# Gated attention and token-MLP mix: shared PSUM banks, a choice of evacuation engine and new planned costs, three weight slots, and MLP1 ahead of the late projections

## The chip, the cores and the metric

The kernel runs on one core of one Trainium2 chip. The metric is the device time of one execution in microseconds, as the median of several executions. The span in a profile (first to last instruction) is about 2 us shorter than that time.

A single core has no die to compare with, so runs are compared by their granted TensorE clock. Runs over 1.5% above the fastest were marked slow and are left out of the ratios. A ratio below is the mean time of one kernel's fast runs over that of the other's fast runs of the same rounds on the same chip, so it is not quite the ratio of the medians quoted beside it, and neither is corrected for the clock. Where a difference is small, runs at like clock are compared as well.

Names: PE is TensorE, PEld its weight loads, DVE is VectorE, ACT is ScalarE, POOL is GpSimd.

## The reference

Sequence S = 2048, width D = 448, 16 heads of 28, 4 segments of 512 rows, MLP width F = 1792. All tensors are bf16.

```python
x = A_x
g = sigmoid((x * gate_w).sum(-1, keepdims=True))
a = attention_with_memory(x, wq, wk, wv, wo, beta)     # below
b = token_mlp(x, w1, b1, w2, b2)                       # below
return g * a + (1 - g) * b

# attention_with_memory, for each segment s (q, k, v are projections of x, per head):
logits = qs @ ks.T * Dh**-0.5 + causal_mask
a_dot  = softmax(logits) @ vs
a_mem  = phi(qs) @ M / (phi(qs) @ z + 1e-6)            # phi(t) = t + 1 if t > 0 else exp(t)
o      = sigmoid(beta) * a_mem + (1 - sigmoid(beta)) * a_dot
M, z   = M + phi(ks).T @ vs, z + phi(ks).sum(0)        # segment s + 1 needs segment s
# ... output projection with wo

# token_mlp mixes along the sequence, so it needs only the normalised x:
h = layernorm(x)
u = gelu(h.T @ w1 + b1)      # MLP1: 14 tiles of 16 matmuls, 128x448 each
y = (u @ w2 + b2).T          # MLP2: 16 tiles of 14 matmuls, 128x448 each
```

What matters here is that the two branches meet only at the end. The MLP is pure TensorE work with light post-processing. Attention is done in 16 units (4 segments by 4 groups of 4 heads) and keeps DVE, ACT and GpSimd busy.

## The kernel before

The kernel records its operations with their reads, writes, cost estimate and priority. A list scheduler then simulates five in-order engines and fixes the order of each engine's instructions at build time. On the chip each engine runs its list in that order and waits on semaphores. So a wrong cost estimate does not break anything: it only puts an instruction at a place in its list where it will wait, and everything behind it on that engine waits too.

The planner, cut:

```python
HOP = 80.0                                   # one figure for every engine-to-engine signal
SWITCH = 110.0

class Sched:
    def op(self, eng, fn, reads=(), writes=(), ..., cost=100.0, lat=None, prio=None, mode=None, nbytes=0):
        ...
        o.cost = cost
        o.lat = {"PE": 180.0, "ACT": 95.0}.get(eng, 0.0) if lat is None else lat
        o.prio = (self.now if prio is None else prio, o.idx)
    def plan(self):
        # ... cut: take the engine that can start first; on it, the ready operation of lowest prio
            o.start = t
            free[e] = t + c
            ...
                o.end = t + c + o.lat
            # ... cut
                r = (o.end + HOP) if (isdep and x.eng != o.eng) else (o.end if isdep else free[e])

def pe_cost(*cols):                 return sum(max(c, 64) / 2.4 + 3.0 for c in cols)
def act_cost(n, sbuf=False, ptr=0): return n / 1.2 + (100.0 if sbuf else 80.0) + 90.0 * ptr
def dve_cost(n, rate=1.0):          return n / rate / 0.96 + 150.0
def pool_cost(n):                   return n / 1.2 + 320.0
```

PSUM banks and engines are fixed when the operation is recorded. Scores own banks 0 to 3, the probability-times-V product (P·V) bank 4, memory term and output projection bank 5, projections alternate between 5 and 6 after the start, the MLP uses 7 (later 6 and 7):

```python
    P_BASE, P_ATT, P_PROJ, P_WO, P_M1, P_M2 = 0.0, 100.0, 200.0, 300.0, 400.0, 500.0   # lower goes first
    CTX, MISC = 4, 5

    def do_k(tc, hg):                      # tc: segment, hg: group of heads
        b = next_bank()
        proj_d(wk_pad, R_wkp, hg, tc, b)   # 4 matmuls, prio=P_PROJ + tc
        op("ACT", lambda e: e.activation(ks, bank(b)[:, 0:512], ACT.Copy), ..., cost=act_cost(512), prio=P_BASE)

    def do_q(tc, hg):
        b = next_bank()
        proj_d(wq_pad, R_wqp, hg, tc, b)
        op("DVE", lambda e: e.tensor_copy(qs, bank(b)[:, 0:512]), ..., cost=dve_cost(512), prio=P_BASE)
```

The clamp of phi, on DVE, and the causal mask, on GpSimd:

```python
        op("DVE", lambda e: e.tensor_scalar_min(kphi[:, p, :], kphi[:, p, :], 1.0), ..., cost=dve_cost(512, 4), ...)
        ...
            op("POOL", lambda e, d=d: e.affine_select(d, d, pattern=[[0, 4], [1, 128]], ...), ..., cost=750, prio=pr)
```

The MLP weights stream through seven slots, four of which reuse memory that the projections own until they are finished, so all projections must come before MLP1 can go far:

```python
    slots = [wown[:, 0, :], wown[:, 1, :], wown[:, 2, :], xTf[:, 0:RING], xTf[:, RING : 2 * RING],
             wqk.rearrange("p a c d -> p (a c d)"), phk.rearrange("p t k -> p (t k)")[:, 0:RING]]
    ...
    def mlp_next():
        i = NFT + NT - len(mlp)
        f_, a = mlp.pop(0)
        f_(a, 7 if i < NB7 else 6 + i % 2)             # bank
        if (i < NFT and i % 2 == 1) or (i >= NFT and (i - NFT) % 2 == 1):
            ring_load()
```

By priority, attention units come first, then projections in segment order, then output projection, MLP1, MLP2. TensorE takes an MLP matmul only when nothing of the rest is ready in the plan.

The softmax here doesn't subtract the row's maximum and nothing guards it: scores larger than these inputs give would overflow.

Of the kernel before, what the change touches and what calls it, by code (L numbers as in the profile page):

```python
# [38 lines left out]
class Op:  # L39
    __slots__ = ("eng", "evspace", "fn", "deps", "order", "is_event", "ev_val", "knowledge", "waits", "name", "idx",  # L40
                 "cost", "lat", "prio", "mode", "start", "end", "pos", "nbytes")
# [3 lines left out]
HOP = 80.0  # L45
SWITCH = 110.0


class Sched:
# [3 lines left out]
    def __init__(self, nc):  # L53
        self.nc = nc
        self.ops = []
        self.per_eng = {e: [] for e in ENGINES}
        self._dma_uid = 0
        self.out_spaces = set()
        self.now = 0.0

    def op(self, eng, fn, reads=(), writes=(), name=None, dma=False, out=False, cost=100.0, lat=None, prio=None,
           mode=None, nbytes=0):
# [4 lines left out]
        o.lat = {"PE": 180.0, "ACT": 95.0}.get(eng, 0.0) if lat is None else lat  # L67
        o.prio = (self.now if prio is None else prio, o.idx)
        o.mode = mode
        o.nbytes = nbytes  # L70
        o.start = o.end = o.pos = None
        if dma:
            self._dma_uid += 1
            o.evspace = "dma_u%d" % self._dma_uid
            o.is_event = True
        else:
            o.evspace = eng
# [12 lines left out]
        for r in reads:  # L90
            if r.last_write is not None:
                need(r.last_write)
            if r.psum and eng != "PE":
                for rd in r.reads:
                    if rd.eng != eng and rd.eng != "PE":
                        need(rd)
# [16 lines left out]
    def plan(self):  # L113
        import heapq
# [3 lines left out]
        ready = [0.0] * len(self.ops)  # L118
# [6 lines left out]
        chan = 0.0  # L125
        waiting = {e: [] for e in ENGINES}
        avail = {e: [] for e in ENGINES}
        for o in self.ops:
            if left[o.idx] == 0:
                heapq.heappush(waiting[o.eng], (0.0, o.prio, o))  # L130
        done = 0
        line = []
        while done < len(self.ops):
            best = None
            for e in ENGINES:
                w, a = waiting[e], avail[e]
                while w and w[0][0] <= free[e]:
                    t, p, o = heapq.heappop(w)
                    heapq.heappush(a, (p, o))
                if a:  # L140
                    t = free[e]
                elif w:
                    t = w[0][0]
                else:
                    continue
                if best is None or t < best[0]:
                    best = (t, e)
            t, e = best
            if not avail[e]:
                while waiting[e] and waiting[e][0][0] <= t:  # L150
                    _, p, o = heapq.heappop(waiting[e])
                    heapq.heappush(avail[e], (p, o))
            _, o = heapq.heappop(avail[e])
            c = o.cost
            if e == "PE" and o.mode != mode:
                c += SWITCH
                mode = o.mode
            o.start = t
            free[e] = t + c
# [3 lines left out]
            else:  # L163
                o.end = t + c + o.lat
            o.pos = done
            line.append(o)
            self.per_eng[e].append(o)
            done += 1
            for x in succ[o.idx]:
                isdep = any(d is o for d in x.deps)  # L170
                r = (o.end + HOP) if (isdep and x.eng != o.eng) else (o.end if isdep else free[e])
# [3 lines left out]
                if left[x.idx] == 0:  # L175
                    heapq.heappush(waiting[x.eng], (ready[x.idx], x.prio, x))
# [52 lines left out]
def pe_cost(*cols):  # L229
    return sum(max(c, 64) / 2.4 + 3.0 for c in cols)  # L230


def act_cost(n, sbuf=False, ptr=0):
    return n / 1.2 + (100.0 if sbuf else 80.0) + 90.0 * ptr


def dve_cost(n, rate=1.0):
    return n / rate / 0.96 + 150.0


def pool_cost(n):
    return n / 1.2 + 320.0


def build_kernel(nc, X, WQ, WK, WV, WO, BETA, W1, B1, W2, B2, GW, OUT):
    sch = Sched(nc)
# [22 lines left out]
    def bank(b):  # L269
        return ps[:, b, :]  # L270


    wown = sb([128, 3, RING])
# [48 lines left out]
    xTf = xT.rearrange("p c t -> p (c t)")  # L322
    slots = [wown[:, 0, :], wown[:, 1, :], wown[:, 2, :], xTf[:, 0:RING], xTf[:, RING : 2 * RING],
             wqk.rearrange("p a c d -> p (a c d)"), phk.rearrange("p t k -> p (t k)")[:, 0:RING]]
# [13 lines left out]
    R_own = R("own", 3)  # L338
# [11 lines left out]
    slot_res = [[R_own[0]], [R_own[1]], [R_own[2]], [r for t in R_xT for r in t], [r for t in R_xT for r in t],  # L350
                [R_wkp, R_wqp], [r for t in R_phk for r in t]]
    R_slot = R("slot", 7)
# [32 lines left out]
    def ring_load():  # L385
# [4 lines left out]
        r = k % 7  # L390
        first = slot_res[r] if k < 7 else []
        if k < 7:
            op("SP", lambda e: e.dma_start(slots[r].rearrange("p (t f) -> p t f", t=NT),
                                           w1v[:, :, k * 256 : k * 256 + 256]),
               reads=[R_wv, R_gw], writes=[R_slot[r]] + first, name=f"ldw1_{k}", dma=True, cost=500,
               nbytes=1048576)
        else:
# [3 lines left out]
               writes=[R_slot[r]] + first, name=f"ldw2_{j}", dma=True, cost=500, nbytes=917504)  # L401
# [31 lines left out]
    P_BASE, P_ATT, P_PROJ, P_WO, P_M1, P_M2 = 0.0, 100.0, 200.0, 300.0, 400.0, 500.0  # L433


    rr = [0]
    banks_now = [[0, 1, 2, 3, 4, 5, 6, 7]]

    def next_bank():
        rr[0] += 1  # L440
        return banks_now[0][(rr[0] - 1) % len(banks_now[0])]

    def fn_warm(e):
        last = None
        for _ in range(18):
            last = e.matmul(bank(7)[:, 0:512], warm[:, 0:128], warm[:, 0:512], start=True, stop=True,  # L446
# [3 lines left out]
    op("PE", fn_warm, reads=[R_ob[0]], writes=[R_bank[7]], name="warm", mode="f", cost=3600, prio=-1)  # L450
# [3 lines left out]
       reads=R_P[0], writes=[R_wkp], name="padk", cost=dve_cost(1792, 2), prio=P_BASE)  # L454

    def pad_q():
        op("DVE", lambda e: e.tensor_copy(wq_pad.rearrange("p c (h j) -> p (c h) j", j=32)[0:CK, :, 0:DH],
                                          wq_nat.rearrange("p c (h j) -> p (c h) j", j=DH)[0:CK]),
           reads=R_P[1], writes=[R_wqp], name="padq", cost=dve_cost(1792, 2), prio=P_BASE)

    def transposes(tc):
        for half in range(2):
            b = next_bank()
            tb = bank(b).bitcast(BF16)

            def fn(e, half=half, tb=tb):
# [9 lines left out]
            op("PE", fn, reads=R_x[4 * tc : 4 * tc + 4] + [R_ident], writes=[R_bank[b]], name=f"trx{tc}_{half}",  # L476
               mode="f", cost=8 * 66, prio=P_PROJ)
            dst = xT[0:CK, 2 * half : 2 * half + 2, tc * 512 : tc * 512 + 512]
            src = tb[0:CK, :].rearrange("p (c t) -> p c t", c=2)
            if tc == 0 and half == 0:  # L480
                op("ACT", lambda e, dst=dst, src=src: e.activation(dst, src, ACT.Copy), reads=[R_bank[b]],
                   writes=[R_xT[tc][half]], name=f"xTcp{tc}_{half}", cost=act_cost(1024), prio=P_BASE)
            else:
                op("DVE", lambda e, dst=dst, src=src: e.tensor_copy(dst, src), reads=[R_bank[b]],
                   writes=[R_xT[tc][half]], name=f"xTcp{tc}_{half}", cost=dve_cost(1024, 2), prio=P_PROJ + tc - 150)

    def proj_d(w_pad, R_w, hg, tc, b):
        def fn(e):
# [7 lines left out]
        op("PE", fn, reads=R_xT[tc] + [R_w], writes=[R_bank[b]], name=f"prd{tc}_{hg}", mode="f",  # L496
           cost=pe_cost(512, 512, 512, 512), prio=P_PROJ + tc)

    def do_k(tc, hg):
# [4 lines left out]
           reads=[R_bank[b]], writes=[R_kT[hg][tc]], name=f"cpk{tc}_{hg}", cost=act_cost(512), prio=P_BASE)  # L504

    def do_kphi(tc, hg):
# [5 lines left out]
           reads=[R_kphi[p]], writes=[R_kphi[p]], name=f"mk{tc}_{hg}", cost=dve_cost(512, 4), prio=P_PROJ + tc)  # L512
        op("DVE", lambda e: e.scalar_tensor_tensor(kphi[:, p, :], ks, 0.0, kphi[:, p, :], op0=ALU.max, op1=ALU.add),  # L513
           reads=[R_kT[hg][tc], R_kphi[p]], writes=[R_kphi[p]], name=f"phk{tc}_{hg}", cost=dve_cost(512),
# [5 lines left out]
    def do_q(tc, hg):  # L520
# [3 lines left out]
        op("DVE", lambda e: e.tensor_copy(qs, bank(b)[:, 0:512]), reads=[R_bank[b]], writes=[R_qT[hg][tc]],  # L524
           name=f"cpq{tc}_{hg}", cost=dve_cost(512), prio=P_BASE)

    def do_qphi(tc, hg):
# [5 lines left out]
           reads=[R_phq[hg][tc]], writes=[R_phq[hg][tc]], name=f"mq{tc}_{hg}", cost=dve_cost(512, 4),  # L533
           prio=P_PROJ + tc)
        op("DVE", lambda e: e.scalar_tensor_tensor(ph, qs, 0.0, ph, op0=ALU.max, op1=ALU.add),  # L535
           reads=[R_qT[hg][tc], R_phq[hg][tc]], writes=[R_phq[hg][tc]], name=f"phq{tc}_{hg}", cost=dve_cost(512),
           prio=P_PROJ + tc)

    def do_v(t):
        b = next_bank()  # L540

        def fn(e):
            last = None
            for c in range(NCT):
# [4 lines left out]
        op("PE", fn, reads=R_xT[t // 4] + [R_wv, R_gw], writes=[R_bank[b]], name=f"prt{t}", mode="f",  # L549
           cost=pe_cost(449, 449, 449, 449), prio=P_PROJ + t // 4)  # L550
        op("ACT", lambda e: e.activation(vaug[:, t, :].rearrange("p (h c) -> p h c", h=H)[:, :, 0:DH],  # L551
                                         bank(b)[:, 0:D].rearrange("p (h c) -> p h c", h=H), ACT.Copy),
           reads=[R_bank[b]], writes=[R_v[t]], name=f"cpv{t}", cost=act_cost(448), prio=P_BASE)
        op("ACT", lambda e: e.activation(gth[:, t : t + 1], bank(b)[:, D : D + 1], ACT.Tanh, scale=0.5),
           reads=[R_bank[b]], writes=[R_gth[t]], name=f"gt{t}", cost=act_cost(1), prio=P_BASE)

    def do_mst(s):
        b = next_bank()

        def fn(e):  # L560
# [9 lines left out]
        op("PE", fn, reads=R_phk[s] + R_v[4 * s : 4 * s + 4], writes=[R_bank[b]], name=f"mst{s}", mode="f",  # L570
           cost=16 * 64, prio=P_PROJ + s)
        mps = bank(b)[:, 0:512].rearrange("p (g c) -> p g c", g=NHG)
        if s == 0:
            op("DVE", lambda e: e.tensor_copy(mst_f32[:], mps), reads=[R_bank[b]], writes=[R_mstf], name="msta0",
               cost=dve_cost(512), prio=P_BASE)
        else:
            op("DVE", lambda e: e.tensor_tensor(mst_f32[:], mps, mst_f32[:], op=ALU.add), reads=[R_bank[b], R_mstf],
# [350 lines left out]
```

## Time and profile before

| | kernel before |
|---|---|
| time, median (lowest to highest) | 210.63 us (209.08 to 210.69), 3 runs |
| profiled span, mean granted clock | 208.8 us, 0.984 |
| busy: PE, DVE, ACT, POOL | 91%, 73%, 65%, 35% |
| matmuls after the last P·V group | 202, in 38.4 us |

Lines of the kernel before that the profile names: L491 is the q and k projection, L711 is P·V, L757 the output projection, L774 MLP1, L799 MLP2, L804 the final combination, L524 the q copy, L511 and L513 phi on DVE, L688 the mask on GpSimd.

From the page of the kernel before: the first lines are the busy times and the busy share in tenths in 40 slices of 5.2 us each, then the chain of work that ended last by engine, then three groups (busy us, mean ns of one | idle before, and its main releaser).

```profile
span 208.8 us, 3428 instructions
...
PE 189.4 (91%) x1359; PEld 84.8 (41%) x1359; DVE 153.4 (73%) x301; ACT 136.7 (65%) x181; POOL 73.7 (35%) x93
...
PE   7799989967996799789778899999999999999994
...
DVE  2779999999999899999999577777657571222222
...
PEclk9999999999999799969999999999999999999999
...
PE 46%; DVE 40%; ACT 7%; POOL 3%; issue 2%
...
L774 PE MATMUL t<-t 128*128 128x448 bf16 x224 | 52.6, 360 | 1.7 <-ACT t L781 1.7
L799 PE MATMUL t<-t 128*128 128x448 bf16 x224 | 43.4, 353 | 0.0
L491 PE MATMUL t<-t 112*128 112x512 bf16 x128 | 31.8, 389 | 6.9 <-DVE t L524 5.0
```

PE seems full at 91%, yet that row stretches matmuls: the groups show 360 and 353 ns for one of 448 columns. The Trainium skill, "Perfetto Trace Analysis", section "Identifying the Most-Contended Engine", comes to the same conclusion: matmul busy time is a bad measure of how close one is to the limit. Its reason, that pipelined matmuls look smaller in a trace, isn't what these groups show; here they look longer than the 189 ns found next. The last lines of the chain of waits of the kernel before show what a matmul really takes (start, us, what, number of instructions):

```profile
166.93 0.66 PE t L711 x16
167.58 5.59 PE t L799 x29
173.18 3.03 PE t L757 x16
176.20 29.71 PE t L799 x157
...
205.94 0.68 DVE t L804
```

157 matmuls in 29.71 us are 189 ns each, half of the 353. From such back-to-back rates the prediction below works out some 178 us of true TensorE work, so about 27 us of the span are gaps. The chain also shows the tail: after the last P·V group (it ends at 167.6 us) there are 29 + 16 + 157 = 202 matmuls and nothing else.

The busy time of each engine in stretches of the kernel before (us of the stretch; then busy us of PE, PEld, DVE, ACT, POOL with counts; granted clock; DMA share; GB/s):

```profile
core 0: us, PE busy (x) PEld busy (x) DVE busy (x) ACT busy (x) POOL busy (x), PEclk, DMA share, GB/s
40.00:50.00 10.00, 7.13 (x58) 2.72 (x57) 9.69 (x25) 7.81 (x10) 3.43 (x4) 1.00 0.13 26
60.00:70.00 10.00, 7.34 (x45) 2.72 (x45) 9.72 (x20) 8.29 (x13) 2.74 (x4) 1.00 0.13 26
88.00:90.00 2.00, 0.43 (x3) 0.25 (x4) 1.93 (x6) 2.00 (x3) 0.13 (x1) 1.00 0.41 78
92.00:94.00 2.00, 2.00 (x13) 0.59 (x11) 2.00 (x4) 1.05 (x2) 1.60 (x2) 0.50 0.92 242
130.00:140.00 10.00, 9.76 (x77) 4.17 (x75) 7.44 (x13) 9.75 (x12) 6.21 (x7) 1.00 0.47 135
180.00:190.00 10.00, 10.00 (x54) 5.19 (x53) 2.19 (x4) 0.00 (x0) 0.00 (x0) 1.00 0.14 46
```

At 40 to 50 and at 60 to 70 us DVE is 97% busy and PE 71 to 73%: TensorE waits for DVE. At 130 to 140 PE and ACT are both nearly full. At 180 to 190 there is only PE, and DVE and ACT have no work. The limit moves from DVE to ACT and PE to PE alone.

One more thing in the timeline of the kernel before (start, duration, engine, line, operation): the same clamp of 128x512 elements takes two different times.

```profile
41.24 0.29 DVE L511 TENSOR_SCALAR t<-t 128x512 bf16<-128x512 bf16 x1
...
41.57 1.18 POOL L688 TENSOR_SCALAR_AFFINE_SELECT t<-t 128x512 bf16<-128x512 bf16 x1 [2.52 <-ACT t L684]
...
42.17 0.72 DVE L511 TENSOR_SCALAR t<-t 128x512 bf16<-128x512 bf16 x1
```

The first clamp runs without a GpSimd instruction beside it and takes 0.29 us. The second starts while the mask L688 runs and takes 0.72. Over the 12 clamps of that line the least is 0.25 and the most 1.37 us. The Trainium skill, "SBUF — State Buffer", section "Who interferes with whom", describes an exclusive lock on a port pair that DVE and GpSimd share; this trace agrees in effect.

### The profile page before, as it was taken

Reading aid. Unit: us, or ns where it says so; the run is one execution under the profiler, and the core shown is the slowest. Engines: PE = TensorE matmul, PEld = TensorE weight load, DVE = VectorE, ACT = ScalarE, POOL = GpSimd, SP = SyncE. Lnnn points to the kernel's source line nnn. Section 1 sums busy time; section 2 is a strip of 40 time slices with the busy share of each in tenths; the row PEclk is TensorE's granted clock in tenths of the full one; section 3 lists DMA queues with packets and bytes.
Section 4 is the critical chain, followed back from the end, with each engine's and each line's share of the span. In section 5 each row is a group of like instructions: output and inputs, shape, how many; then the busy total and the mean of one; then the engine's idle time right before and its main releaser. Section 6 shows DMA issues by size and latency. Waiting matters only on the chain.

```text
span 208.8 us, 3428 instructions
## 1 busy us (share of the span) xinstructions
PE 189.4 (91%) x1359; PEld 84.8 (41%) x1359; DVE 153.4 (73%) x301; ACT 136.7 (65%) x181; POOL 73.7 (35%) x93
## 2 busy tenths in 40 slices
PE   7799989967996799789778899999999999999994
PEld 2446434323532244333333344334343455555551
DVE  2779999999999899999999577777657571222222
ACT  2262799995998779959859799998899405000000
POOL 8100058450424123744473652763745520000000
PEclk9999999999999799969999999999999999999999
DMA  5999901020202079774407153260606160111111
GB/s 157 255 286 287 276 8 25 5 50 12 41 0 50 19 209 223 202 206 110 121 0 202 36 141 99 80 176 3 176 0 179 51 191 22 49 44 44 44 44 44
DMA packets 42451, 21.75 MB, mean 104 GB/s; under 512 B 7876, under 2 KB 42436, under 8 KB 42436
## 3 DMA queue, kind: packets, MB, share of 16 engines
q1 hardware_dynamic: 41496, 21.30, 38.5%
q10 hardware_dynamic: 940, 0.24, 0.5%
q8 instruction: 10, 0.16, 0.3%
q14 instruction: 5, 0.04, 0.1%
HBM read 18.13 MB, written 1.84 MB: 96 GB/s over the span
## 4 chain that ended last, share of the span: by engine, by line
PE 46%; DVE 40%; ACT 7%; POOL 3%; issue 2%
PE t L799 20%; PE t L491 6%; PE t L757 5%; PE t L774 4%; ACT t L684 4%; DVE t L513 3%; DVE t L734 3%; DVE t L725 3%; DVE t L535 3%; PE t L711 3%; DVE t L744 3%; PE t L446 3%; DVE t L639 3%; DVE t L736 3%; DVE t L724 2%; DVE t L511 2%
## 5 line engine op out<-in xcount | busy, mean ns | idle before, releaser
L684 ACT ACTIVATE t<-t 128x2048 bf16<-128x2048 f32 (+1 forms) x48 | 77.6, 1616 | 5.3 <-PE t L675 5.0
L688 POOL TENSOR_SCALAR_AFFINE_SELECT t<-t 128x512 bf16<-128x512 bf16 x64 | 47.6, 750 | 70.6 <-ACT t L684 69.3
L774 PE MATMUL t<-t 128*128 128x448 bf16 x224 | 52.6, 360 | 1.7 <-ACT t L781 1.7
L799 PE MATMUL t<-t 128*128 128x448 bf16 x224 | 43.4, 353 | 0.0
L491 PE MATMUL t<-t 112*128 112x512 bf16 x128 | 31.8, 389 | 6.9 <-DVE t L524 5.0
L774 PEld LDWEIGHTS t<-t 128*128 128x128 bf16 x224 | 20.4, 99 | 24.7 <-issue 8.1
L804 DVE SCALAR_TENSOR_TENSOR t<-t 128x448 bf16<-128x448 f32 x16 | 10.8, 677 | 26.5 <-PE t L799 26.4
L799 PEld LDWEIGHTS t<-t 128*128 128x128 bf16 x224 | 21.6, 98 | 20.3 <-issue 0.5
L738 POOL TENSOR_TENSOR t<-t 128x512 bf16<-128x512 f32 x12 | 17.5, 1456 | 26.5 <-DVE t L736 26.5
L491 PEld LDWEIGHTS t<-t 112*128 112x128 bf16 x128 | 11.1, 99 | 22.0 <-DVE t L524 5.8
L675 PE MATMUL t<-t 28*128 28x512 bf16 (+3 forms) x256 | 17.5, 306 | 1.2 <-ACT t L684 1.2
L763 ACT ACTIVATE t<-t 128x448 bf16<-128x448 f32 x16 | 11.7, 731 | 9.7 <-PE t L757 9.6
L757 PE MATMUL t<-t 128*128 128x448 bf16 x64 | 14.3, 355 | 4.0 <-DVE t L724 3.8
L725 DVE STREAM_TRANSPOSE t<-t 128x512 f32<-128x512 f32 x16 | 11.4, 710 | 5.9 <-PE t L711 5.9
L744 DVE STREAM_TRANSPOSE t<-t 128x512 bf16<-128x512 bf16 x16 | 11.3, 706 | 4.6 <-POOL t L738 4.4
L545 PE MATMUL t<-t 112*128 112x449 bf16 x64 | 14.5, 361 | 0.0
L711 PE MATMUL t<-t 128*32 128x512 bf16 (+3 forms) x256 | 12.3, 316 | 1.4 <-POOL t L688 1.3
L551 ACT ACTIVATE t<-t 128x448 bf16<-128x448 f32 x16 | 8.7, 562 | 7.4 <-PE t L545 7.4
L675 PEld LDWEIGHTS t<-t 28*128 28x128 bf16 x256 | 5.2, 92 | 19.3 <-ACT t L684 12.4
L524 DVE CAST t<-t 128x512 bf16<-128x512 f32 x16 | 10.8, 678 | 1.5 <-PE t L491 1.4
L503 ACT ACTIVATE t<-t 128x512 bf16<-128x512 f32 x16 | 10.0, 651 | 2.9 <-PE t L491 2.9
L623 DVE BATCH_NORM_STATS2 t<-t 128x6 f32<-128x448 bf16 x16 | 9.5, 597 | 2.6 <-DMA t<-in_A_x_dram 2.6
(75 smaller groups left out, 214.9 us busy)
## 6 DMA issues: line engine op xcount, KB each, us to landing
t<-in_B_w_dram SPq DMA_DIRECT2D x7, 1024.0 KB, 7.2
t<-in_B_w_dram SPq DMA_DIRECT2D x8, 896.0 KB, 5.2
out_dram<-t SPq DMA_DIRECT2D x16, 112.0 KB, 1.7
t<-in_A_x_dram SPq DMA_DIRECT2D x3, 448.0 KB, 9.3
t<-in_A_wk_dram SPq DMA_DIRECT2D x1, 392.0 KB, 5.0
t<-in_A_wq_dram SPq DMA_DIRECT2D x1, 392.0 KB, 6.9
t<-in_A_wv_dram SPq DMA_DIRECT2D x1, 392.0 KB, 8.2
t<-in_A_wo_dram SPq DMA_DIRECT2D x4, 98.0 KB
```

Of the source, the lines that this page charges most:

```text
L491: last = e.matmul(bank(b)[:, 0:512], w_pad[0:CK, c, hg * 128 : hg * 128 + 128], xT[0:CK, c, tc * 512 : tc * 512 + 512], start=(c == 0), st ...
L545: last = e.matmul(bank(b)[:, 0 : D + 1], xT[0:CK, c, t * 128 : t * 128 + 128], wvx[0:CK, c, :], start=(c == 0), stop=(c == NCT - 1), skip_ ...
L675: last = e.matmul(bank(hl)[:, c0 : c0 + w_], kT[r, hg, s * 512 + j * 128 : s * 512 + j * 128 + 128], qT[r, hg, s * 512 + 128 * j : s * 512 ...
L684: op("ACT", lambda e: e.activation(pv, ps[:, 0:4, 0:w], ACT.Exp, scale=SCALE), reads=R_bank[0:4], writes=[R_P[u % 2][f]], name=f"exp{n}", ...
L688: op("POOL", lambda e, d=d: e.affine_select(d, d, pattern=[[0, 4], [1, 128]], compare_op=ALU.is_ge, fill=0.0, base=0, channel_multiplier=- ...
L711: last = e.matmul(bank(CTX)[32 * hl : 32 * hl + 32, 128 * j : 512], vaug[:, 4 * s + j, 32 * h : 32 * h + 32], pv[:, hl, c0 : c0 + w_], sta ...
L725: dv(lambda e: e.transpose(t2[:, 0, :], bank(CTX)[:, 0:512]), [R_bank[CTX]], [R_tt[tb][0]], "ta", 720)
L738: op("POOL", lambda e: e.tensor_tensor(o, t2[:, 0, :], t2[:, 1, :], op=ALU.add), reads=R_tt[tb], writes=[R_ob[tb]], name=f"o{u}", cost=140 ...
L744: dv(lambda e: e.transpose(oT[:, hg, s * 512 : s * 512 + 512], o), [R_ob[tb]], [R_qT[hg][s]], "ot", 700)
L757: last = e.matmul(bank(b)[:, 0:D], oT[:, hg, T * 128 : T * 128 + 128], wo_sb[:, hg, :], start=(hg == 0), stop=(hg == NHG - 1), skip_group_ ...
L774: op("PE", lambda e, st=st: e.matmul(bank(b)[:, 0:D], w1c[:, st, f2 * 128 : f2 * 128 + 128], xh[:, st, :], start=(st == 0), stop=(st == NT ...
L799: op("PE", lambda e, ft=ft: e.matmul(bank(b)[:, 0:D], w2c[:, ft, t2_ * 128 : t2_ * 128 + 128], uT[:, ft, :], start=(ft == 0), stop=(ft == ...
```

## The change

The intent is to fill TensorE's gaps in the first 110 us with MLP work and so shorten the tail. Three things are done for it.

1. **Order.** The projections of segments 2 and 3 get priorities inside the MLP instead of before it, so MLP1 starts earlier. Because the memory of those projections is then not free, the weight slots shrink from seven to three of their own.
2. **Planner resources.** Projections, P·V, memory term, output projection and MLP take a bank from a pool of four (4 to 7) when the plan reaches them, and most PSUM evacuations may go to ACT or DVE, whichever is free first in the plan.
3. **Planner costs.** The cost figures are set nearer to measured ones, engine-to-engine hops get a table, and a new rule lets operations flagged `port` on DVE and GpSimd exclude each other in the plan.

No arithmetic changes. The diff, cut to its core:

```diff
-HOP = 80.0
-SWITCH = 110.0
+HOP = {("PE", "ACT"): 40.0, ("PE", "DVE"): 40.0, ("ACT", "PE"): 58.0, ("DVE", "PE"): 60.0, ... }
+SWITCH = 97.0
+LAT = {"PE": 163.0, "ACT": 120.0, "DVE": 83.0, "POOL": 50.0, "SP": 0.0}
 ...  plan():
+            if o.take is not None:                       # bank given out when the plan reaches the operation
+                b = min((v[0], b) for b, v in banks.items())[1]
+                o.take.bank = b
+                o.deps = o.deps + banks[b][1]
+                banks[b] = (1e18, [])
+            o.eng = e                                     # engine chosen by the plan among o.alts
+            o.fn, c, pt = o.alts[e]
+            if pt:                                        # DVE and GpSimd exclude each other
+                t = max(t, port)
+                port = t + c
 ...
 def act_cost(n, sbuf=False, ptr=0):
-    return n / 1.2 + (100.0 if sbuf else 80.0) + 90.0 * ptr
+    return n / 1.2 + (95.0 if sbuf else 50.0) + 92.0 * ptr
 def dve_cost(n, rate=1.0):
-    return n / rate / 0.96 + 150.0
+    return n / rate / 0.96 + 70.0
 ...
-    slots = [wown[:, 0, :], ..., xTf[:, 0:RING], xTf[:, RING : 2 * RING], wqk..., phk...]
+    slots = [wown[:, i, :] for i in range(NSL)]          # NSL = 3
 ...
+    PRJ = (P_PROJ, P_PROJ + 1, P_M1 + 8.5, P_M2 + 4.5)
 ...
-           cost=pe_cost(512, 512, 512, 512), prio=P_PROJ + tc)
+           cost=pe_cost(512, 512, 512, 512), prio=PRJ[tc])
 ...  do_q():
-        op("DVE", lambda e: e.tensor_copy(qs, bank(b)[:, 0:512]), ...)
+        op("DVE", lambda e: e.tensor_copy(qs, bank(b)[:, 0:512]), **buse(b), ...,
+           alt=("ACT", lambda e: e.activation(qs, bank(b)[:, 0:512], ACT.Copy), act_cost(512)))
 ...  masks:
-               ..., name=f"mask{n}_{c0}", cost=750, prio=pr)
+               ..., name=f"mask{n}_{c0}", cost=590, port=True, prio=pr)
 ...  ln_coef(): the power (rstd) on GpSimd
-            op("POOL", fn, ..., cost=250, prio=P_BASE)
+            op("POOL", fn, ..., cost=2900 if name == "rstd" else 200, prio=P_BASE)
 ...  pv_unit(), wo_tile(), mm1(), mm2():
-    CTX, MISC = 4, 5
+        mb, cb = Bank("pool"), Bank("pool")
```

## The prediction

> **What bounds the kernel now.** The span is 208.8 us, matmul busy 91%, but that row stretches matmuls: the groups show 353 to 360 ns for 448 columns, while in the unbroken run ending the chain of waits 157 take 29.71 us, 189 ns each. The chain's back-to-back rates (189 ns MLP and output projection, 221 for 512-column projections, 193 for V, 0.7 us per probability-times-V group, 0.9 us per unit's scores) over all counts give about 178 us of true TensorE work; with 4 us of start and end the floor is near 182: 27 us are gaps.
>
> In the 10 us windows DVE is 90 to 99% busy from 20 to 110 us while four PE windows are only 71 to 78%; there the chain is nearly all DVE. From 110 to 160 us PE and ACT share the limit (both about 95%), DVE about 74%. From 167.6 us there is PE only: 202 matmuls, 38 us.
>
> **What the change does.** Same arithmetic.
> - Projections of segments 2 and 3 go behind MLP1 and into MLP2. After the last attention unit 118 matmuls remain, 22.3 us instead of 38.2.
> - Evacuations: ACT takes 3 more x-transpose copies and 11 q copies; DVE takes 8 k copies, 7 v copies, 5 GELU halves, 6 gate evacuations. With the group means DVE gains about 7 us (153 to 161), ACT loses about 7 (137 to 130). It helps by timing only.
> - Four shared banks instead of fixed ones remove waits such as TensorE on q copies (5.0 us, weight loads 5.8, in the waits).
> - Three weight slots instead of seven: a 1 MB load lands in 7.2 us, a 0.9 MB one in 5.2; two tiles use a slot for at least 5.3 us, with two slots ahead: nearly no wait.
>
> **Sum along the path.** I cut both orders at each unit's output transpose and add durations (scaled to the busy union, 0.93 on DVE). Before: DVE to unit 8 105 us plus 7 of idle start, then PE 89.5, plus 3: 205, against 208.8 measured, so stalls cost 4. After: DVE to unit 11 119 plus 7, then PE 64.4, plus 3, plus 4 of stalls: 197.5. Planned costs nearer to measured ones should trim stalls. They include DVE-GpSimd exclusion, which the Trainium skill, "SBUF — State Buffer", describes as an exclusive lock on a shared port pair; the trace agrees: the same 512-element clamp takes 0.25 us at best and 0.72 us beside a GpSimd mask.
>
> **Prediction: 196 us, 189 to 205 in 8 of 10.** Faster by over 2%: 0.89; within 2%: 0.09; slower: 0.02.
>
> **What would show it.** A PE-only tail of 22 to 25 us (38 before). DVE over 90% from 20 to about 125 us, then near 65%; DVE total about 161 us, ACT 130. PE busy 94 to 97%. TensorE's waits on q copies under 3 us. No wait over 2 us on a weight load.
>
> **What would make it wrong.** (a) DVE growing more than 7 us through lock conflicts: 200 or over. (b) In-order engines stalling where durations differ from the plan, or units 12 to 15 held by ACT's exponentials with no MLP2 tile to fill: plus 5. (c) The load queue blocked behind a slot, delaying phi transposes or weights: plus 3 to 6. (d) The granted clock, 0.83 in two windows now, dropping in a denser run: plus 2 to 4. (e) DVE keeping pace better than its means: 189.

## More of the kernel before

The mean clock of an execution of this kernel is between 0.975 and 1.0, and the time follows it: over all executions the kernel before took about 209.0 us at clock 1.0, 209.4 at 0.991, 210.6 at 0.984 and 213.5 at 0.976.

The two short stretches at 88 and 92 us show another loss: PE is busy for only 0.43 us of 2, and shortly after the granted clock is 0.50.

## The result, and the profile after

| | before | after |
|---|---|---|
| time, median (lowest to highest) | 209.86 us (208.93 to 210.69), 4 runs | 193.66 us (191.93 to 194.31), 4 runs |
| ratio of fast runs, 95% interval | | 0.9216 (0.9138 to 0.9295) |
| profiled span, clock | 208.8 us, 0.984 | 191.8 us, 0.991 |
| at clock 1.0 | about 209.0 us | 191.93 us (one run) |
| matmuls after the last P·V group | 202, in 38.4 us | 118, in 22.5 us |

The result is correct; the kernel before has one run more here than above, made beside it. The kernel takes 7.8% less time. At clock 1.0 the difference is 17 us (one run of the kernel after); at 0.991 it is about 15.5 (193.9, the mean of three runs, against 209.4).

In the kernel after, L558 is the q and k projection, L788 P·V, L836 the output projection, L856 MLP1, L884 MLP2, L890 the final combination, L550 the copy of transposed x, L675 the tanh of beta. The page of the kernel after, the same parts as before:

```profile
span 191.8 us, 3430 instructions
...
PE 184.2 (96%) x1350; PEld 85.1 (44%) x1359; DVE 157.0 (82%) x313; ACT 134.0 (70%) x169; POOL 74.3 (39%) x93
...
PE   7769999999999999999999999999999999999993
...
DVE  2678987989999998989888997898899998971221
...
PEclk9988999999999999999999999999999999999999
...
PE 87%; DVE 4%; DMA 3%; ACT 3%; issue 1%; ACTq 1%
...
L856 PE MATMUL t<-t 128*128 128x448 bf16 x224 | 48.4, 354 | 0.5 <-DVE t L579 0.2
L884 PE MATMUL t<-t 128*128 128x448 bf16 x224 | 45.1, 353 | 0.1
L558 PE MATMUL t<-t 112*128 112x512 bf16 x128 | 31.6, 396 | 2.7 <-DVE t L550 2.7
```

PE's row is at 9 from the fourth slice to the last but one, and the chain, formerly 46% PE and 40% DVE, is now 87% PE. The projection's idle time on q copies (5.0 us before) is gone; what remains of it is one wait of 2.7 us at the start. DVE's row stays at 7 to 9 from 10 to about 170 us.

The chain of waits of the kernel after, its start and its end:

```profile
1.85 6.63 DMA t<-in_A_beta_dram
8.51 0.22 ACT t L675
...
10.21 0.70 DVE t L550
...
11.05 7.03 PE t L558 x24
...
165.80 0.66 PE t L788 x16
166.45 6.54 PE t L884 x34
172.99 3.03 PE t L836 x16
176.02 12.88 PE t L884 x68
188.92 0.68 DVE t L890
```

The tail after the last P·V group is 34 + 16 + 68 = 118 matmuls in 22.5 us, at the same 189 ns each.

The same windows of the kernel after, with two short ones from its start (columns as before):

```profile
10.00:12.00 2.00, 0.95 (x5) 0.51 (x6) 1.77 (x6) 0.00 (x0) 0.00 (x0) 1.00 1.09 373
12.00:14.00 2.00, 2.00 (x8) 0.79 (x7) 1.28 (x6) 1.24 (x3) 0.00 (x0) 0.63 1.12 301
40.00:50.00 10.00, 10.00 (x90) 4.11 (x89) 9.10 (x19) 9.19 (x11) 4.69 (x6) 1.00 0.16 44
60.00:70.00 10.00, 9.79 (x74) 4.43 (x74) 9.82 (x19) 9.64 (x11) 4.00 (x5) 1.00 0.09 19
130.00:140.00 10.00, 9.95 (x56) 5.01 (x55) 8.63 (x16) 1.75 (x2) 3.67 (x4) 1.00 0.73 172
```

PE is full or nearly so (98 to 100%) where it was 71 to 73%, at about the same DVE load (91 to 98%, against 97). From 130 to 140 us ACT has little to do and DVE is at 86%.

**Where the 17 us came from.** The path can be cut at two places that both chains show. From the first projection to the last matmul the kernel before needs 9.67 to 205.9 us, 196.2 in all, and the kernel after 11.05 to 188.9, 177.9 in all: 18.4 us less. The first projection starts 1.4 us later. The end after the last matmul is 2.9 us in both. The sum is −17.0 us, the difference of the spans. Of the prediction's estimate of 178 us of true TensorE work about 171 lie in that stretch (without the 6.1 us of warm-up and 0.9 of first transposes), so the gaps in it fell from about 25 us to about 7. These gaps include what the half-clock stretches cost: the profiled execution before had two of them (clock 0.984), the one after had one (0.991), so by estimate some 1.7 of the 17 us are the clock.

Attention itself hardly moved: the last P·V group ends at 167.6 us before and at 166.5 after. The gain is the 84 matmuls (202 less 118) that now lie in the gaps before it; at 189 ns they are 15.9 us.

**The one thing that grew.** The start of the chain after shows it. The tanh of beta stands in ACT's list ahead of the first copy of x, and it waits until 8.51 us for the load of beta. DVE's small operations that depend on it are ahead of the other copy (L550). So the projections begin at 11.05 instead of 9.67. In the windows PE is busy for 0.95 us of the 2 from 10 to 12, and the granted clock is 0.63 in the next 2.

### The profile page after: what moved, and what is told of

It reads as the page before. It is cut to its first block, busy times and chain, and to the rows that moved or that the text cites. A ratio compares the mean times of both kernels' runs of the same rounds, so it can differ in the third digit from the quotient of the medians.

```text
span 191.8 us, 3430 instructions
## 1 busy us (share of the span) xinstructions
PE 184.2 (96%) x1350; PEld 85.1 (44%) x1359; DVE 157.0 (82%) x313; ACT 134.0 (70%) x169; POOL 74.3 (39%) x93
## 4 chain that ended last, share of the span: by engine, by line
PE 87%; DVE 4%; DMA 3%; ACT 3%; issue 1%; ACTq 1%
PE t L884 23%; PE t L856 21%; PE t L558 16%; PE t L751 7%; PE t L614 7%; PE t L836 6%; PE t L788 5%; DMA t<-in_A_beta_dram 3%; PE t L638 2%; ACT t L760 2%; PE t L539 1%; DVE t L803 1%; DVE t L604 1%; ACT t L860 1%; PE t L774 0%
## 5 line engine op out<-in xcount | busy, mean ns | idle before, releaser
L764 POOL TENSOR_SCALAR_AFFINE_SELECT t<-t 128x512 bf16<-128x512 bf16 x64 | 49.6, 779 | 52.8 <-ACT t L760 42.2
L856 PE MATMUL t<-t 128*128 128x448 bf16 x224 | 48.4, 354 | 0.5 <-DVE t L579 0.2
L884 PE MATMUL t<-t 128*128 128x448 bf16 x224 | 45.1, 353 | 0.1
L558 PE MATMUL t<-t 112*128 112x512 bf16 x128 | 31.6, 396 | 2.7 <-DVE t L550 2.7
L884 PEld LDWEIGHTS t<-t 128*128 128x128 bf16 x224 | 21.2, 98 | 20.6 <-issue 1.4
L856 PEld LDWEIGHTS t<-t 128*128 128x128 bf16 x224 | 19.9, 98 | 19.9 <-issue 3.0
L816 POOL TENSOR_TENSOR t<-t 128x512 bf16<-128x512 f32 x12 | 16.3, 1357 | 23.4 <-DVE t L814 23.4
L890 DVE SCALAR_TENSOR_TENSOR t<-t 128x448 bf16<-128x448 f32 x16 | 10.8, 676 | 14.8 <-PE t L884 14.7
L558 PEld LDWEIGHTS t<-t 112*128 112x128 bf16 x128 | 12.1, 101 | 18.1 <-issue 5.5
L842 ACT ACTIVATE t<-t 128x448 bf16<-128x448 f32 x10 | 7.2, 724 | 9.7 <-PE t L836 9.5
L614 PE MATMUL t<-t 112*128 112x449 bf16 x64 | 13.6, 355 | 0.0
L836 PE MATMUL t<-t 128*128 128x448 bf16 x64 | 13.6, 353 | 0.0
L594 ACT ACTIVATE t<-t 128x512 bf16<-128x512 f32 x11 | 6.6, 596 | 10.0 <-PE t L558 10.0
L822 DVE STREAM_TRANSPOSE t<-t 128x512 bf16<-128x512 bf16 x16 | 11.1, 693 | 0.8 <-POOL t L816 0.8
L788 PE MATMUL t<-t 128*32 128x512 bf16 (+3 forms) x256 | 11.6, 302 | 0.0
L868 DVE SCALAR_TENSOR_TENSOR t<-t 128x448 f32<-128x448 f32 x14 | 10.6, 758 | 0.3 <-ACT t L863 0.3
L581 DVE SCALAR_TENSOR_TENSOR t<-t 128x512 bf16<-128x512 bf16 x12 | 10.6, 884 | 0.0
```

The lines of the kernel that those rows point to most:

```text
L558: last = e.matmul(bank(b)[:, 0:512], w_pad[0:CK, c, hg * 128 : hg * 128 + 128], xT[0:CK, c, tc * 512 : tc * 512 + 512], start=(c == 0), st ...
L614: last = e.matmul(bank(b)[:, 0 : D + 1], xT[0:CK, c, t * 128 : t * 128 + 128], wvx[0:CK, c, :], start=(c == 0), stop=(c == NCT - 1), skip_ ...
L788: last = e.matmul(bank(cb)[32 * hl : 32 * hl + 32, 128 * j : 512], vaug[:, 4 * s + j, 32 * h : 32 * h + 32], pv[:, hl, c0 : c0 + w_], star ...
L816: op("POOL", lambda e: e.tensor_tensor(o, t2[:, 0, :], t2[:, 1, :], op=ALU.add), reads=R_tt[tb], writes=[R_ob[tb]], name=f"o{u}", cost=145 ...
L822: dv(lambda e: e.transpose(oT[:, hg, s * 512 : s * 512 + 512], o), [R_ob[tb]], [R_qT[hg][s]], "ot", 635)
L836: last = e.matmul(bank(b)[:, 0:D], oT[:, hg, T * 128 : T * 128 + 128], wo_sb[:, hg, :], start=(hg == 0), stop=(hg == NHG - 1), skip_group_ ...
```

## The experiments

The theory before the first run, called O in the expectations: the order makes the gain, by letting TensorE fill its gaps with the MLP; banks, choice and costs only make it possible and matter for a few microseconds. The rival: the planner (realistic costs and exclusion, free banks, choice of engine) makes the gain, by taking stalls out of an order that could have been about the old one. A third came up on the way: the parts work only together. Each kernel below is the changed kernel with one part undone, except where it is said. All gave correct results. One warning holds for all of them: the planner is greedy, so any edit changes the whole order, and a difference of a microsecond or two can come from that. The diffs are cut to their core.

| run | what | median us | ratio to before (95%) |
|---|---|---|---|
| e1_early_proj | old order, rest changed | 208.13 | 0.989 (0.9795 to 0.9985) |
| e2_no_choice | fixed evacuation engines | 196.72 | 0.9382 (0.9289 to 0.9476) |
| e3_banks_by_kind | no sharing of banks between kinds | 196.75 | 0.9382 (0.9303 to 0.9461) |
| e5_before_late_proj | kernel before, with order and three slots | 217.0 | 1.0339 (1.0265 to 1.0412) |
| e4_old_costs | old cost figures, no exclusion | 208.14 | 0.9926 (0.9852 to 1.0001) |
| e7_banks_as_e5 | changed kernel, banks as in e5 | 209.81 | 0.9953 (0.9873 to 1.0033) |
| e10_old_costs_no_choice | order and bank pool only | 207.7 | 0.9876 (0.9824 to 0.9928) |
| e6_late_beta | tanh of beta planned later | 193.41 | 0.9205 (0.9137 to 0.9273) |
| e11_pow_cost_old | one cost figure back | 194.8 | 0.9285 (0.9214 to 0.9355) |
| e12_old_costs_pow | old costs but for that figure | 207.42 | 0.9871 (0.9802 to 0.994) |
| e13_beta_moved | same plan, beta moved by hand | 191.75 | 0.9131 (0.9087 to 0.9175) |
| e14_no_lock | new costs, no exclusion in the plan | 202.84 | 0.9676 (0.9596 to 0.9755) |

The medians mix clocks, and the kernel after has only one run at clock 1.0 (191.93 us) and three at 0.991 (mean 193.9). Against these, at like clock, e2 is slower by 3.9 us, e3 by 4.7, e11 by 2.6, e14 by 10, e4 by 14 to 16, e7 by 15 to 16 and e6 by about 1; e13 is level at clock 1.0. Runs of e1 and e10 have no like clock in the kernel after; against the kernel before at 0.983 to 0.984 (210.6 us) e1 is faster by 4.6 us (one run) and e10 by 3.0.

### Undo the order alone

```diff
-    PRJ = (P_PROJ, P_PROJ + 1, P_M1 + 8.5, P_M2 + 4.5)
+    PRJ = (P_PROJ, P_PROJ + 1, P_PROJ + 2, P_PROJ + 3)
```

> The changed kernel with the projections of segments 2 and 3 put back ahead of MLP1 (their old priorities), all else as changed. Theory O (order: the gain comes from spreading the DVE work of the late projections over MLP1 and MLP2): 202 to 209 us, TensorE windows of 70 to 85% come back between 40 and 110 us with DVE above 90%, and a matmul-only tail of over 35 us. Rival B (shared banks give the gain) and rival E (choice of engine for each evacuation gives it): 193 to 197 us, as both are kept.

It took 208.13 us: costs, pool, choice and three slots without the order are worth only 2.5 us (4.6 at like clock). So the order is necessary. This kernel keeps the three slots, but no wait of TensorE on the arrival of MLP weights shows in its trace, so they are not seen to hold it; the old order with seven slots under the new planner was not run. Where the gaps would be was expected wrongly. Windows of this kernel (columns as before):

```profile
130.00:140.00 10.00, 7.12 (x62) 2.81 (x60) 8.68 (x15) 9.42 (x11) 5.27 (x7) 1.00 0.53 144
140.00:150.00 10.00, 8.45 (x64) 3.50 (x65) 6.28 (x11) 5.33 (x5) 5.27 (x7) 0.66 0.25 59
150.00:160.00 10.00, 7.79 (x49) 2.94 (x46) 8.58 (x19) 2.90 (x4) 1.91 (x3) 1.00 0.04 13
```

PE is at 99% or more from 20 to 90 us here and has its gaps at 90 to 100 and above all at 130 to 165; the last P·V group is done at about 151 us, and the MLP follows as a tail of about 53. In the second line the clock is 0.66, following the gaps of the first.

### Undo the choice of engine

```diff
+        if name == "xTcp0_0":            # the one copy that was on ACT before
+            eng, fn, cost = alt
+            ...
+        alt = None                       # everything else on its old engine
```

> The changed kernel with every evacuation back on its fixed engine of before (q and x-transpose copies on DVE, k, v, GELU halves and gate on ACT), all else as changed. Theory O: 194 to 198 us, DVE total down by about 4 to 7 us. Rival E: 202 us or more, with TensorE waiting for evacuations. Rival B: 193 to 198 us.

It took 196.72 us, 3 more than the changed kernel (3.9 at like clock). DVE's busy total fell to 151.8 us, so the choice does put work on DVE, as the prediction said, and helps a little all the same.

### Undo the sharing of banks, keep the rest

```diff
+    def __init__(self, name, may=(4, 5, 6, 7)):
+        self.may = may
-                b = min((v[0], b) for b, v in banks.items())[1]
+                b = min((v[0], b) for b, v in banks.items() if b in o.take.may)[1]
-        return Bank("pool")              # projections
+        return Bank("pool", (5, 6))
-        mb, cb = Bank("pool"), Bank("pool")
+        mb, cb = Bank("pool", (5,)), Bank("pool", (4,))      # memory term, P.V
-        b = Bank("pool")                 # MLP1, MLP2; output projection gets (5,)
+        b = Bank("pool", (6, 7))
```

> The changed kernel, but each kind of tile may take only the banks that it had before (projections and state 5 or 6, memory read and output projection 5, attention 4, MLP 6 or 7), still given out in planned order. Theory O: 194 to 199 us. Rival B (sharing of the four banks): 202 us or more, with TensorE waits on copies and evacuations of 5 us and over.

It took 196.75 us. Each kind may use only its old banks, but the plan still gives them out when it reaches the operation. That keeps all but 3 us of the gain (all but 4.7 at like clock), so the free pool as such is not what most of the gain rests on.

### The order in the kernel before

This starts from the kernel before. The MLP needs banks while projections are still to come, so projections of segments 2 and 3 got bank 6, MLP1 bank 7, and the memory states bank 5.

```diff
+    PRJ = (P_PROJ, P_PROJ + 1, P_M1 + 8.5, P_M2 + 4.5)
-           cost=pe_cost(512, 512, 512, 512), prio=P_PROJ + tc)
+           cost=pe_cost(512, 512, 512, 512), prio=PRJ[tc])
-        r = k % 7
+        r = k % 3
+        if tc > 1:
+            banks_now[0] = [6]
-    NB7 = 4
+    NB7 = 19
```

> The kernel before, with its old planner, old costs, fixed engines and fixed banks, given only the new order of priorities and the three-slot ring; as fixed banks tie the orders together, the late projections have bank 6 alone, MLP1 and the first five MLP2 tiles bank 7 alone, and the state product is recorded just before the units that need it. Theory O: 196 to 204 us. Rival B: 205 us or more, since one bank for MLP1 makes TensorE wait for each GELU evacuation, and in this form the order cannot be had without the pool.

It took 217.0 us, slower than the kernel before. TensorE's waits show scores on exponentials with 7.7 us (another 20.9 on their weight loads). But this kernel differs from the changed one in several ways at once (single banks, banks fixed when recorded, fixed engines, old costs), so it could not tell which of them hurt. The next runs take up the costs and the single banks one at a time.

### Old cost figures in the changed kernel

```diff
-SWITCH = 97.0
-LAT = {"PE": 163.0, "ACT": 120.0, "DVE": 83.0, "POOL": 50.0, "SP": 0.0}
+SWITCH = 110.0
+LAT = {"PE": 180.0, "ACT": 95.0, "DVE": 0.0, "POOL": 0.0, "SP": 0.0}
-    return HOP.get((a, b), 80.0)
+    return 0.0 if a == b else 80.0
-            if pt:
+            if False:
# ... and each cost= back to its old figure
```

> The changed kernel whose planner is given the old cost figures, hand-over times and no DVE-GpSimd exclusion; order of priorities, pool and choice of engine stay. Theory O with the first runs (order 10 us of the 17 at equal clock, choice and sharing 3 to 4 each): 193 to 197 us. Rival C (the measured costs carry the gain, since in-order engines stall where the plan is off): 200 us or more.

It took 208.14 us, so theory O failed here (it expected 193 to 197): with order, pool and choice all in place and only the plan's figures old, 14.5 of the 16 us are lost. The tail is even shorter, about 83 matmuls after the last P·V group, and yet the kernel is slower: the gaps have come back before it, as two windows show (columns as before).

```profile
60.00:70.00 10.00, 8.01 (x67) 3.27 (x63) 9.86 (x18) 9.40 (x13) 2.94 (x4) 1.00 0.46 118
70.00:80.00 10.00, 8.04 (x78) 3.46 (x70) 9.83 (x16) 7.59 (x7) 4.83 (x5) 1.00 0.50 124
```

The timeline of this kernel shows the plainest gap (a bracket gives the idle time of the engine before the instruction and what ended it):

```profile
29.26 3.28 POOL L710 TENSOR_TENSOR t<-t 128x16 f32<-128x16 f32 x1
...
33.17 1.93 DVE L716 TENSOR_SCALAR t<-t 128x448 bf16<-128x448 bf16 x3 [3.41 <-POOL t L713]
...
34.40 0.73 PE L788 MATMUL t<-t 128*32 128x512 bf16 x16 [2.70 <-POOL t L764]
```

The power for the layer norm takes 3.28 us on GpSimd; the plan believed 0.25. DVE stands for 3.41 us until the coefficients computed from it are there (L713), whatever else its list holds behind that place, and TensorE's P·V stands for 2.70 until the masks have run that are queued behind the power on GpSimd.

### The single banks in the changed kernel

```diff
-        b = next_bank()                            # do_k, do_q (and do_v alike)
+        b = next_bank((5, 6) if tc < 2 else (6,))
-        b = Bank("pool", (6, 7))                   # MLP1 (MLP2's first five tiles too), on top of e3_banks_by_kind
+        b = Bank("pool", (7,))
```

> The changed kernel with the narrow banks that the old kernel needed for the new order (late projections bank 6 alone, MLP1 and the first five MLP2 tiles bank 7 alone, state product 5), given out in planned order. If single banks are what made the new order slow on the old kernel (217.0 us): 205 us or more here too. If not (old costs, fixed engines or the recorded order of banks did it): 195 to 201 us.

It took 209.81 us against e3_banks_by_kind's 196.75. One bank instead of two for the late projections and for MLP1 costs 13 us (about 11 at like clock). So two banks for these kinds are necessary; whether kinds share them matters less. The reason, that with one bank a tile's matmuls cannot start until the tile before is evacuated, is argued from the program: the trace puts only 2.3 us of waiting matmuls and 2.4 of weight loads on GELU evacuations, and the waits of scores' weight loads on exponentials grow from 11.1 to 15.6 us. How the 13 us split was not taken apart.

### Order and pool only

```diff
# the edits of e4_old_costs and e2_no_choice together
```

> The changed kernel with the old costs and fixed engines together: what is left of the change is the order, the three-slot ring and the four shared banks. If order plus pool carry the gain: 196 to 201 us. If they need the costs or the choice: 203 us or more.

It took 207.7 us, so order and bank pool alone are worth 3 us. Together with e1_early_proj, where all but the order is worth 2.5, this is the third theory: the two halves bring 5.5 us apart (7.6 at like clock) and 16 together.

### Is it that one cost figure?

```diff
# e11_pow_cost_old: the power alone back
-cost=2900 if name == "rstd" else 200
+cost=200
# e12_old_costs_pow: e4_old_costs, with the power at its measured figure
-cost=250
+cost=2900 if name == "rstd" else 250
```

> The changed kernel with one planned cost put back: the power function of layernorm on GpSimd at 200 ns instead of 2900 (2.9 us in both traces). If this one entry is what the old costs broke (theory C1): 201 us or more, with GpSimd masks and the layernorm applies held behind the power function. If the loss of the old costs is spread over many entries (C2): 193 to 197 us.

> The changed kernel with all old costs except the power function, which is planned at 2900 ns. C1: 193 to 198 us. C2: still 202 us or more. Both at once: 198 to 202 us.

The first took 194.8 us, about 1 more than the changed kernel (2.6 at like clock); the second 207.42, less than 1 below e4_old_costs. So the gap that looked worst in the timeline is not where the 14 us went. It was an argument from one picture, and the runs refuted it.

### The exclusion alone

```diff
-            if pt:
+            if False:
```

> The changed kernel whose planner no longer keeps DVE instructions and GpSimd instructions that share the port pair apart in time; all single costs stay as measured. If the old costs lost 14 us because the exclusion was missing from the plan: 200 us or more. If they lost it through many durations and hand-overs together: 193 to 197 us.

It took 202.84 us (201.76 to 204.06): the rule is worth about 9 of the 14 us (10 at like clock), if the parts add up. Busy totals of this kernel, and its largest wait of TensorE on GpSimd:

```profile
PE 185.7 (93%) x1359; PEld 84.8 (42%) x1359; DVE 157.5 (79%) x318; ACT 133.2 (66%) x164; POOL 73.7 (37%) x93
```

```profile
PE t L788 <- POOL t L764: 2.3, 2, 1.2
```

DVE and POOL are busy for 157.5 and 73.7 us, against 157.0 and 74.3 in the kernel after. So the rule does not save locked time. What it changes is that the plan counts the lock: P·V's matmuls and their weight loads wait 2.3 and 7.9 us on masks here, where the kernel after has no such matmul wait and 1.8 us on the loads. Other waits grew too: ACT's exponentials wait 13.4 us on scores, against 7.4.

### The late start

```diff
# e6_late_beta: let the plan start the tanh of beta at 9.5 us, and replan
-           name="tb", cost=200, prio=pr)
+           name="tb", cost=200, prio=pr, rel=9500.0)
# e13_beta_moved: keep the plan; behind the first x copies, put tanh of beta and what depends on it
+    moved = [o for o in line[: last + 1] if o.name == "tb"]
+    # ... and each later operation up to there that depends on one of them
+    line = [o for o in line[: last + 1] if o not in moved] + moved + line[last + 1 :]
```

> The changed kernel with the small tanh of beta held in the plan until 9.5 us, so that it and the DVE instructions behind it no longer stand ahead of the first x-transpose copies while beta's load is under way until 8.5 us (trace of the changed kernel). The first projection should start at 9.3 to 9.7 us instead of 11.05; as TensorE is nearly gapless after that, the span should shrink by 1.3 to 1.8 us: 191.5 to 192.5 us in the median, if the replanned rest is as good.

> The changed kernel with its planned order kept instruction for instruction, but for the tanh of beta and the eight or so small DVE instructions that hang on it, which are moved behind the first x-transpose copies. First projection at 9.3 to 9.7 us instead of 11.05. As TensorE is gapless later, nearly all of that shows if nothing else holds TensorE: median 192.0 to 192.6 us; if DVE's saturation up to 130 us is what really paces the middle, less than 0.5 us shows.

Both start the projections at 9.4 us. The replanned one took 193.41 us, no real gain: its new order has PE at 9.1 to 9.5 of 10 us in three later windows where the kernel after is nearly full. e13_beta_moved, with the rest of the plan kept, took 191.75 us (191.42 to 192.39 in 6 runs), the fastest kernel, ratio 0.9131 to before. All 6 runs had a clock of 0.998 or more, while three of four runs of the kernel after had 0.991. Against the one run of the kernel after at clock 1.0 (191.93 us) the difference is only 0.2 us. That is the second outcome that its expectation named (less than 0.5 us), and its trace shows where the time went: from 10 to 40 us PE is busy for 28.8 of 30 us, where the kernel after has no gap from 20 to 40, so most of the earlier start is lost again there. What its median gains is then likely the half-clock stretch that no longer follows the late start; one run at clock 1.0 is not enough to call that shown.

### What was not run

A ring of four slots did not build, because the memory did not fit: three slots follow from keeping the projections' data alive. A ring of two was not run. What of the old costs makes up the 5 us beyond the exclusion was not taken apart.

## Why the prediction was right, and where it was not

**Right, by the measure it named.** The time (193.66 against 196, range 189 to 205) and the direction. The tail of 22.5 us (22 to 25 predicted). PE busy 96% (94 to 97). TensorE's waits on q copies are 1.6 us, all of weight loads for scores (under 3 predicted); no wait of TensorE on the arrival of MLP weights shows, so three slots were enough. The main mechanism (not the sum along the path, see below), MLP matmuls moving from the tail into the gaps, is what the chain shows: 84 of them, at 189 ns, are 15.9 of the 17.0 us.

**"Planned costs nearer to measured ones should trim stalls" was mis-sized, and badly.** The sum kept 4 us of stalls and gave this 1.5 us at most. With the old figures the kernel loses 14.5 us (e4_old_costs), and the exclusion alone is worth about 9 (e14_no_lock). The prediction took the order that the planner would write for granted and summed durations along it. But the gain lies in an order that the in-order engines can follow without stalling, and that depends on the figures. It held the cost table for a refinement, where it was one of three necessary parts.

**"DVE to unit 11 119 plus 7, then PE 64.4" described the path wrongly.** 87% of the chain after is PE, nearly gapless from 11 us on; DVE has 4% of it. Unit 11 (units count from 0) has the twelfth output transpose, L822, in the timeline of the kernel after:

```profile
144.51 0.70 DVE L822 STREAM_TRANSPOSE t<-t 128x512 bf16<-128x512 bf16 x1
```

It ended at 145.2 us, not 126: until then DVE was busy for 128.0 us (119 predicted) and idle for 17 (7 predicted), so DVE alone did not set that time. Only 46.6 us of the span remained, not 67.4 (64.4 plus 3) nor the 4 us of stalls. An error of +19 us and one of −25 brought the sum near the measurement, and that was luck. A total that fits does not confirm its terms.

**"DVE total about 161 us" was too high.** It gained 3.6 us (153.4 to 157.0), about half of the 7 predicted; ACT fell by 2.7 and not 7. "Then near 65%" was wrong as well: DVE is at 86 to 100% from 130 to 170 us, since the late projections and their phi now come there.

**Fear (d), a lower clock in a denser run, has the wrong sign.** In the traces the half-clock stretches follow gaps: at 66 to 70 and 88 to 90 us before, at 8 to 11 after, at 136 to 142 in e1_early_proj. The Trainium skill, "TensorE: Matmul & The Clock Gate", section "Part 1: The HAM clock gate", states just that: TensorE's clock is halved after an idle window of about 3.4 us and restored after a busy one. The traces agree in depth (0.50 in the slice at 92 us of the kernel before, 0.52 from 14 to 16 us after) and in length (in both kernels, two or three neighbouring slices of 2 us whose shortfalls make up about 3.4 us at half clock and cost about 1.7; in e1_early_proj it is twice that), but not in the length of the gap needed (see the closing list). A fuller TensorE had less of it.

**Not foreseen: the late start.** The diff does not show that the tanh of beta would move ahead of a copy on the path; the instruction lists did. It put off the first projection by 1.4 us, and a half-clock stretch followed in the profiled run; at clock 1.0 the run without it (e13_beta_moved) was only 0.2 us faster.

**What stays open.** The choice of engine, the sharing of banks and the power's figure came out at 1 to 3 us each in the medians and at 2.6 to 4.7 at like clock. The two runs with beta show that the same idea can differ by 1.7 us through replanning alone, so the sizes of these three are not firm.

## What to carry to other kernels

When the limiting engine changes along a kernel, count the work that waits in the last regime and ask how much of it fits into the gaps of the first; this is what the Trainium skill, "Perfetto Trace Analysis", section "Optimization Strategy", advises with interleaving regimes, and here it gave 16 us for no arithmetic, though only with the planner's other parts. With in-order engines and a plan made at build time, the order pays only if the plan knows the real durations, including who locks out whom, and, for the late projections and the MLP, has two buffers per kind to plan with: order and pool alone brought 3 us, the rest alone 2.5. Test parts both alone and left out, and don't trust the worst gap in a timeline until a run without it is measured.

## What the Trainium skill lacked or had wrong

- "SBUF — State Buffer", section "Who interferes with whom", has the rule of the lock, but not that a static plan has to count it. Here leaving it out of the plan cost 9 us (202.84 against 193.66) with nearly equal busy totals of both engines, so the loss does not show in those but as waits, TensorE's among them.
- "TensorE: Matmul & The Clock Gate", section "HAM oscillation — how this bites in real kernels", puts the rule as no idle gaps over about 3.4 us; the section after it tells of short idles that were enough in another kernel, without their lengths. Here shorter ones were enough: PE stood still for 2.7 us at once before 11.05 us, and a clock of 0.63 and then 0.52 followed; in the kernel before, TensorE was busy for 1.82 of the 4 us from 66 to 70 us, in pieces (2.17 us idle at once), and 0.58 followed. The same late start left the clock at 1.0 in the trace of e14_no_lock, with 2.64 us idle at once, so the length alone does not decide; this fits the page's remark that the window runs freely, which no run here tests.
- No page that I found has the time of an elementwise power on GpSimd: 128x16 f32 elements took 2.92 us in the kernel before and 3.28 in e4_old_costs, where a multiply of the same shape took 0.22.
- "Perfetto Trace Analysis", section "Optimization Strategy", says that interleaving regimes may help, and not what that depends on. Here the interleaved order alone, put into the kernel before with the three slots and single banks that it needed there, was 3.4% slower (217.0 us).
